# Clustered attention into a SiLU feed-forward: reciprocals moved from VectorE to GpSimd as a power, and the first round's steps and the tail put in another order

## The chip, the cores and the metric

The kernel runs on one core of a Trainium2 chip. A core has engines that run at the same time, each with its own queue in program order: TensorE (PE, matmuls; PEld are its weight loads), VectorE (DVE), ScalarE (ACT) and GpSimd (POOL), and SP, whose queue here only issues transfers. The transfers themselves run on 16 DMA engines. Results of PE land in PSUM, in a few numbered slots; everything else lives in SBUF. The metric is device microseconds of one execution, median of three runs.

## The reference

Four batches of eight heads, 768 positions, 64 dimensions. Each query and key is assigned to one of 16 clusters; a query attends to the keys of its own cluster. The result goes through a feed-forward layer with SiLU, weights 512 x 2048 and 2048 x 512.

```python
q_assign = np.argmax(np.einsum('bhsd,hcd->bhsc', q_n, c_n), axis=-1)
k_assign = np.argmax(np.einsum('bhsd,hcd->bhsc', k_n, c_n), axis=-1)
mask = q_assign[:, :, :, None] == k_assign[:, :, None, :]
scores = np.where(mask, scale * np.matmul(q, k.transpose(0, 1, 3, 2)), -1000000000.0)
attn = np.exp(scores - np.max(scores, axis=-1, keepdims=True))
attn = attn / (np.sum(attn, axis=-1, keepdims=True) + 1e-09)
x = np.matmul(attn, v)                # then (batch*seq, heads*dim)
h = x @ w_in
out = (h * (1.0 / (1.0 + np.exp(-h)))) @ w_out
```

## The kernel before, in words

**Preparation of queries and keys.** They come as `items`: items 0 to 7 hold one head's keys and the first half of its queries, items 8 and 9 the second halves of batch 0's queries, items 10 on one head each. An item is loaded by SP (`load_qk`, L104; four buffers), split into a high half-precision part on ACT (`hi`, L136) and a low rest on DVE (`lo`, L142), and turned so that the dimension lies on partitions: items 0 to 7 by matmuls with the identity on PE (`pe_tr`, L154) and two copies, ACT's and DVE's (`tr_out`, L164), later ones by a transposing DMA that SP issues (`xpose`, L147). `logits` (L173) are matmuls with the normalised centroids; DVE finds the maximum and makes it one-hot (`am_t`, `am_max`), turns it back (`am_back`) and writes it as extra rows beside the turned queries and keys (`codes`, L230). So the mask comes out of the same matmul as the score.

**Steps.** The work is a list of 192 steps, 6 to a pass and 32 passes. In batch 0 a pass takes two heads and half of the queries (three steps per head), later one head and all queries. In step T the host issues the score matmuls of step T + 1 (`qk_mm`, L252; slot `st` of PSUM, two of them), any preparation on PE, feed-forward units, P times V of an earlier pass (`pv_mm`, L290; one slot), the exponential of step T on ACT (`exp`, L272), the copy out of P times V on DVE (`evac`, L302), and then what else the table `steps` has for T. `at(T, f, ...)` puts it there; within a step the order is that of the calls to `at`. Each engine follows this order, so a waiting instruction holds up all that stand behind it in its queue.

**The row sums' chain.** V carries 64 columns of ones, so P times V gives the row sums too. `evac` has SP spread the sums over 128 partitions (`zt`, 3 KB); `recip` (L315) inverts them on DVE and has SP store them to DRAM (`rzd`); `bcast` (L322) has SP load them back, repeated on 64 partitions (`rzb`, 192 KB); `norm` (L328) multiplies on GpSimd and leaves `xt`, the input of the feed-forward layer. E is the step of a pass's last `evac`: `recip` stands at E + 5, `bcast` at E + 7 and `norm` at E + 9 in batch 0 and the last pass, and one step later in the others.

**Feed-forward.** `unit_a` (L345) is four matmuls into `ph` and, one step later, a tanh on ACT and a product on DVE that leaves `gt`; `unit_b` (L365) is eight matmuls, half of one output tile. They wait in `qa` and `qb` until a batch's `xt` are due (`ready`, L553 and L556) and are mixed into the steps by `pop_mlp` (L386), and what is left comes in a loop after the last step (L586). The weights come in 16 loads that GpSimd issues (`w_load`), each behind a small copy (`pace`) that waits for a given step's exponential. `fill` (L394) issues matmuls on zeros that only keep PE busy.

Of the kernel before, what the change touches and what calls it, by code (L numbers as in the profile page):

```python
# [9 lines left out]
f32 = mybir.dt.float32  # L10
f16 = mybir.dt.float16
AF = mybir.ActivationFunctionType
ALU = mybir.AluOpType
# [4 lines left out]
def kernel(  # L18
# [10 lines left out]
    nc = tc.nc  # L29
    B, H, S, D = q.shape  # L30
# [4 lines left out]
    NJ = S // 128  # L35
    NFB = DF // 128
    NR = DM // 128
    NBH = B * H
# [6 lines left out]
    NSPLIT = H // 2  # L45
# [4 lines left out]
    const = ctx.enter_context(tc.tile_pool(name="const", bufs=1))  # L50
# [9 lines left out]
    ckl = const.tile([128, H, 32], f16, name="ckl")  # L60
    ohp = [const.tile([128, 12, 32], f16, name=f"oh{n}") for n in range(3)]
    ohn = [const.tile([128, 9, 32], f16, name=f"ohn{n}") for n in range(2)]
    pace = const.tile([128, 1], f32, name="pace")
    zz = const.tile([128, 512], f16, name="zz")

# [75 lines left out]
    @per_item  # L141
    def lo(n):  # L142
        ho, lw, src = parts(n)
        nc.vector.scalar_tensor_tensor(out=lw, in0=src, scalar=QS, in1=ho, op0=ALU.mult, op1=ALU.subtract)  # L144
# [9 lines left out]
    def pe_tr(n):  # L154
        hl = hls[n]
        trs[n] = []
        for a, w in ((0, NJ), (NJ, NJ // 2)):
            tag, bufs = ("po", 1) if a == 0 else ("mm", 2)
            pT = ps.tile([128, w * 128], f16, name="pT", tag=tag, bufs=bufs)
            for t in range(w):  # L160
                nc.tensor.transpose(pT[:, 128 * t : 128 * t + 128], hl[:, a + t].rearrange("p c d -> p (c d)"), ident)
            trs[n].append(pT)
# [9 lines left out]
    @per_item  # L172
    def logits(n):  # L173
        ab = abs_[n]
        if n < H:

            psL = ps.tile([128, 9, HC], f32, name="psL9", tag="mm", bufs=2)
            for t in range(9):
                for w, st in ((stk, True), (ckl, False)):
                    nc.tensor.matmul(psL[:, t, :], ab[:, t, :], w[:, order[n], 0:HC], start=st, stop=not st)  # L180
            psLs[n] = psL
            return
        psL = ps.tile([128, HALF], f32, name="psL", tag="mm", bufs=2)
        for w, st in ((stk, True), (ckl, False)):
            for g, (hd, _, _) in enumerate(items[n]):
                nc.tensor.matmul(  # L186
                    psL[32 * g : 32 * g + 32, :], w[:, hd % H, :],
                    ab[:, 3 * g : 3 * g + 3, :].rearrange("p n c -> p (n c)"),
                    start=st, stop=not st,
                )  # L190
        psLs[n] = psL
# [30 lines left out]
    @per_item  # L222
    def am_back(n):
        w = 32 * (9 if n < H else 12)
        ohT = mp.tile([128, HALF], f16, name="ohT", bufs=2)
        nc.vector.transpose(ohT[:, 0:w], oh_of(n).rearrange("p n c -> p (n c)"))  # L226
        ohs[n] = ohT
# [23 lines left out]

    def qk_mm(T):  # L252
        if not 0 <= T < NS:
            return
        p, j = divmod(T, NJ)
        pS = ps.tile([128, 1024], f32, name="pS", tag="st", bufs=2)
        if p < H:
            hd, a = head_of(p, j // 3), 3 * (p // NSPLIT)
            if T < 40 and T % 3 != 2:
                nc.tensor.matmul(pS[:, 0:512], zz[:, 0:128], zz, start=True, stop=True)  # L260
            for t in range(2):
                nc.tensor.matmul(  # L262
                    pS[:, 512 * t : 512 * t + HALF], k_tile(hd, 2 * (j % 3) + t), q_tiles(hd, a, 3),
                    start=True, stop=True,
                )
        else:
            lhsT = k_tile(p, j)
            nc.tensor.matmul(pS[:, 0:512], lhsT, q_tiles(p, 0, 4), start=True, stop=True)  # L268
            nc.tensor.matmul(pS[:, 512:768], lhsT, q_tiles(p, 4, 2), start=True, stop=True)  # L269
        pst[T] = pS  # L270

    def exp(T):  # L272
        if not 0 <= T < NS:
            return
        P = mp.tile([128, S], f16, name="P", bufs=12)
        pS = pst.pop(T)
        if T < NJ * H:
            nc.scalar.activation(  # L278
                out=P.rearrange("p (c x) -> p c x", c=2), in_=pS.rearrange("p (c x) -> p c x", c=2)[:, :, 0:HALF],
                func=AF.Exp, bias=0.0, scale=ESC,  # L280
            )
        else:
            nc.scalar.activation(out=P, in_=pS[:, 0:S], func=AF.Exp, bias=0.0, scale=ESC)  # L283
        Ps[T] = P
# [29 lines left out]

    def recip(p):  # L315
        rz = mp.tile([128, NJ], f32, name="rz", bufs=3)
        nc.vector.reciprocal(rz, zts.pop(p))
        rzd = drpool.tile([S], f32, name="rzd", tag="rzd", bufs=4)
        nc.sync.dma_start(rzd.rearrange("(p c) -> p c", c=NJ), rz)
        rzds[p] = rzd  # L320

    def bcast(p):  # L322
# [13 lines left out]
        )  # L336

    gts = {}
    late = []

    def flush():
        while late:
# [40 lines left out]
    qa, qb = [], []  # L383
# [9 lines left out]

    def fill(n):  # L394
        if n:
            junk = ps.tile([128, 512], f32, name="junk", tag="mm", bufs=2)
            for _ in range(n):
                nc.tensor.matmul(junk, zz[:, 0:128], zz, start=True, stop=True)

# [23 lines left out]
    def at(T, f, *a):  # L423
        steps.setdefault(T, []).append((f, a))
# [57 lines left out]
    nc.vector.tensor_copy(stk[0:64, :, 0:HC], chv)  # L482
    nc.vector.tensor_copy(stk[64:128, :, 0:HC], chv)
    nc.vector.tensor_copy(ckl[0:64, :, 0:HC], pst1[64:128, :].rearrange("d (h c) -> d h c", c=HC))
    fill(3)


    def due(n):
# [6 lines left out]
    for n in range(NI):  # L495
        d = due(n)
        near = n < H + 2
        if n < H:
            first = n == 0
            at(3 * n - 2 - 3 * first, codes, n)  # L500
            at(3 * n - 3 - 3 * first, am_max, n)
            at(3 * n - 3 - 3 * first, am_back, n)
            at(3 * n - 5 - first, logits, n)
            if n > 0:
                at(3 * n - 7, pe_tr, n)
                at(3 * n - 7, tr_out, n)
                at(3 * n - 10, lo, n)
            if n > 1:
                at(3 * n - 12, hi, n)
        else:  # L510
            at(d - 5, am_back, n)
            at(d - 5, codes, n)
            at(d - 6, am_max, n)
            at(d - 7, am_t, n)
            at(d - 8, logits, n)
            x = d - (14 if near else 23)
            at(x, xpose, n)
            at(x - 2, lo, n)
            at(x - 4, hi, n)
        if n > 3:  # L520
            at(d - (24 if near else 40), load_qk, n)
# [4 lines left out]
            at(T - (12 if n < H else 15), load_v, hd)  # L526
        at(T - 6, cast_v, hd)
    for n in range(2 * NW):
        T = 14 * n // 5 - 3

        def gated(T=T, n=n):
            if T > 0:
                nc.gpsimd.tensor_copy(pace, Ps[T][:, 0:1])
            w_load(n)

        at(T, gated)
# [3 lines left out]
    for p in range(NBH):  # L540
        for c in range(2):
            T = pass_at(p, c)
            pv_at[T] = (p, c, range(0, 3))
            pv_at[T + 1] = (p, c, range(3, 6))
            evac_at[T + 2] = (p, c)
        E = T + 2
        near = p < H or p == NBH - 1
        at(E + (5 if near else 6), recip, p)
        at(E + (7 if near else 8), bcast, p)
        N = E + (9 if near else 10)  # L550
        for c in range(2):
            at(N, norm, p, c)
        if p in (NSPLIT - 1, H - 1):  # L553
            ready[N + 3] = [(0, p // NSPLIT)]
        elif p % H == H - 1 and p < NBH - 1:
            ready[N + 3] = [(p // H, 0), (p // H, 1)]  # L556

    for T in range(min(steps), max(steps) + 1):
        p, j = divmod(T, NJ)
        for r in ready.get(T, []):  # L560
            qa.extend((*r, fb) for fb in range(NFB))
        done, late[:] = late[:], []
        qk_mm(T + 1)
        for f, a in steps.get(T, []):
            if f in on_pe:
                f(*a)
        if T >= 0:
            pop_mlp(j, 0.67 if T >= 114 else 0.43 if qb else 0.9)
        if T in pv_at:
            pv_mm(*pv_at[T])  # L570
        exp(T)
        if T in evac_at:
            evac(*evac_at[T])
        for f in done:
            f()
        for f, a in steps.get(T, []):
            if f not in on_pe:
                f(*a)
# [2 lines left out]

    tags = ("mm", "st")
    n = m = 0
    qa.extend((B - 1, 0, fb) for fb in range(NFB))
    qa.extend((B - 1, 1, fb) for fb in range(NFB))
    while qa or qb or late:  # L586
        if qa:
            unit_a(*qa.pop(0), tags[n % 2])
        if qb and (n % 5 in (1, 3) or not qa):
            unit_b(*qb.pop(0), ("po", "pv")[m // 2 % 2])  # L590
            m += 1
        n += 1
        while len(late) > (2 if qa or qb else 0):
            late.pop(0)()
# [28 lines left out]
```

## Time and profile before

| what | value |
|---|---|
| median of three runs | 381.83 us (380.72 to 383.01) |
| profiled execution, its own time | 380.09 us |
| span of that execution | 378.2 us |
| DVE reciprocals L317 | 32, 182 ns each |
| POOL normalisations L334 | 64, 1023 ns each in the mean |
| rzd and rzb together, us to landing (min, median, max) | 1.4, 3.3, 6.9 |
| zt, us to landing (min, median, max) | 2.0, 2.1, 4.7 |
| granted clock, 10 to 20 us | 0.50 |
| granted clock, 70 to 80 us | 0.65 |

An engine's share of busy time is over the whole span; the stages differ. The first 80 us hold the preparation of batch 0 and no feed-forward work; from there to 309 us attention steps and feed-forward units are mixed; after that only feed-forward work is left. A row of the timeline gives start, length, engine, line and operation, and in brackets how long the engine stood idle before it and what ended that. "SPq" rows are transfers being issued; they land later.

### The profile page before, as it was taken

The numbers are of one execution on the slowest core, as the hardware profiler recorded it, in microseconds if no ns is written. First come the engines' busy times: TensorE is split into PE (matmuls) and PEld (weight loads), VectorE is DVE, ScalarE is ACT, GpSimd is POOL, SyncE is SP. The second block draws the span as 40 slices with busy tenths as digits, with TensorE's granted clock in tenths as the row PEclk, the third lists the DMA queues.
The fourth block names the chain that finished last, engine by engine and source line by source line (L and its number), as shares of the span: only waits on it lengthen the run. The fifth ranks groups of instructions, "written<-read, shape, count | busy, mean of one in ns | idle before, by whom it ended". The sixth has DMA issues, their size and how long they took to land.

```text
span 378.2 us, 6204 instructions
## 1 busy us (share of the span) xinstructions
PE 340.9 (90%) x2130; PEld 179.4 (47%) x2130; DVE 257.7 (68%) x579; ACT 234.1 (62%) x367; POOL 97.4 (26%) x144
## 2 busy tenths in 40 slices
PE   6778878559999999999698899999999998899995
PEld 2445434225445554454354555555555554455542
DVE  5777867228896788878798887787667445454531
ACT  6566858438976678767787867677557623343310
POOL 5122253332430222234223232223321222200000
PEclk9588989869999999999999999999999999999999
DMA  6698788989965675569967655443211012010102
GB/s 180 135 218 180 152 118 171 195 179 165 197 156 134 118 177 143 144 155 193 213 104 176 128 126 155 112 112 86 71 52 49 23 50 97 2 55 29 52 32 83
DMA packets 74479, 46.51 MB, mean 123 GB/s; under 512 B 52944, under 2 KB 68304, under 8 KB 74448
## 3 DMA queue, kind: packets, MB, share of 16 engines
q1 hardware_dynamic: 71120, 41.93, 45.9%
q0 software_dynamic: 3328, 4.20, 7.7%
q8 instruction: 16, 0.26, 0.3%
q14 instruction: 15, 0.12, 0.1%
HBM read 33.59 MB, written 6.39 MB: 106 GB/s over the span
## 4 chain that ended last, share of the span: by engine, by line
PE 63%; DVE 19%; DMA 9%; issue 3%; ACT 2%; SPq 2%; POOL 0%; DVEq 0%; ACTq 0%; POOLq 0%
PE po L371 21%; PE ph L352 16%; PE pO L300 12%; PE pS L268 5%; DVE gt L357 3%; DMA zt<-osb 3%; PE pS L269 3%; DMA qk<-in_q_dram 3%; DVE osb L306 2%; PE psL L186 2%; DMA rzb<-rzd 2%; DVE ab L248 2%; PE pS L262 2%; DVE ohT L226 2%; DVE ab L246 2%
## 5 line engine op out<-in xcount | busy, mean ns | idle before, releaser
L283 ACT ACTIVATE P<-pS 128x768 f16<-128x768 f32 x144 | 115.5, 812 | 52.8 <-PE pS L269 52.5
L334 POOL TENSOR_TENSOR xt<-osb,rzb 64x384 f16<-64x384 f32 x64 | 64.4, 1023 | 195.6 <-DMA rzb<-rzd 157.7
L352 PE MATMUL ph<-xt,win_s 128*128 128x384 f16 x512 | 101.9, 328 | 10.0 <-POOL xt L334 7.4
L300 PE MATMUL pO<-P,vt 128*128 128x384 f16 x384 | 85.8, 333 | 8.1 <-DVE osb L306 8.1
L356 ACT ACTIVATE tn<-ph 128x384 f32<-128x384 f32 x128 | 62.6, 489 | 47.5 <-PE ph L352 46.8
L357 DVE SCALAR_TENSOR_TENSOR gt<-tn,ph 128x384 f16<-128x384 f32 x128 | 69.6, 547 | 31.2 <-ACT tn L356 28.1
L371 PE MATMUL po<-wout_s,gt 128*128 128x512 f16 x384 | 89.7, 379 | 0.0
L352 PEld LDWEIGHTS <-win_s 128*128 128x128 f16 x512 | 49.9, 97 | 45.8 <-issue 11.1
L306 DVE COPY osb<-pO 128x384 f32<-128x384 f32 x64 | 35.3, 551 | 34.1 <-PE pO L300 30.9
L371 PEld LDWEIGHTS <-gt 128*128 128x128 f16 x384 | 37.5, 98 | 40.9
L300 PEld LDWEIGHTS <-vt 128*128 128x128 f16 x384 | 35.8, 99 | 41.7 <-issue 20.9
L268 PE MATMUL pS<-ab 80*128 80x512 f16 x144 | 54.8, 381 | 0.3
L278 ACT ACTIVATE P<-pS 128x768 f16<-128x768 f32 x48 | 37.1, 809 | 12.5 <-PE pS L262 11.7
L269 PE MATMUL pS<-ab 80*128 80x256 f16 x144 | 38.9, 270 | 0.0
L144 DVE SCALAR_TENSOR_TENSOR hl<-qk,hl 128x768 f16<-128x768 f32 (+1 forms) x34 | 30.6, 901 | 1.5 <-ACT hl L139 1.2
L378 DVE TENSOR_SCALAR ot<-po 128x512 f32<-128x512 f32 x24 | 16.5, 689 | 18.4 <-PE po L371 18.3
L139 ACT ACTIVATE hl<-qk 128x768 f16<-128x768 f32 (+1 forms) x34 | 27.2, 802 | 1.9 <-DMA qk<-in_q_dram 1.9
L197 DVE STREAM_TRANSPOSE LT<-psL 128x384 f32<-128x384 f32 x26 | 15.1, 579 | 11.1 <-PE psL L186 10.6
L127 POOL CAST vt<-vn 128x384 f16<-128x384 f32 x32 | 16.7, 523 | 17.9 <-DMA vn<-in_v_dram 17.2
L269 PEld LDWEIGHTS <-ab 80*128 80x128 f16 x144 | 14.2, 99 | 11.2 <-issue 0.8
L268 PEld LDWEIGHTS <-ab 80*128 80x128 f16 x144 | 14.0, 97 | 11.1 <-issue 0.3
L248 DVE TENSOR_SCALAR ab<-ohT 16x384 f16<-16x384 f16 x48 | 18.2, 379 | 1.1
(74 smaller groups left out, 226.3 us busy)
## 6 DMA issues: line engine op xcount, KB each, us to landing
qk<-in_k_dram SPq DMA_DIRECT2D x32, 192.0 KB, 3.3
vn<-in_v_dram SPq DMA_DIRECT2D x32, 192.0 KB, 3.4
rzb<-rzd SPq DMA_DIRECT2D x32, 192.0 KB, 3.5
out_dram<-ot SPq DMA_DIRECT2D x24, 256.0 KB, 2.1
qk<-in_q_dram SPq DMA_DIRECT2D x24, 192.0 KB, 3.1
win_s<-in_moe_w_in_dram POOLq DMA_DIRECT2D x8, 256.0 KB, 5.0
wout_s<-in_moe_w_out_dram POOLq DMA_DIRECT2D x8, 256.0 KB, 5.9
qk<-in_q_dram SPq DMA_DIRECT2D x16, 96.0 KB, 3.3
```

What stands on the lines that cost most here:

```text
L144: nc.vector.scalar_tensor_tensor(out=lw, in0=src, scalar=QS, in1=ho, op0=ALU.mult, op1=ALU.subtract)
L268: nc.tensor.matmul(pS[:, 0:512], lhsT, q_tiles(p, 0, 4), start=True, stop=True)
L269: nc.tensor.matmul(pS[:, 512:768], lhsT, q_tiles(p, 4, 2), start=True, stop=True)
L278: nc.scalar.activation(out=P.rearrange("p (c x) -> p c x", c=2), in_=pS.rearrange("p (c x) -> p c x", c=2)[:, :, 0:HALF], func=AF.Exp, bia ...
L283: nc.scalar.activation(out=P, in_=pS[:, 0:S], func=AF.Exp, bias=0.0, scale=ESC)
L300: nc.tensor.matmul(pOs[p, c], vts[hd % H][:, j, :], rhs, start=(j == 0), stop=(j == NJ - 1))
L306: nc.vector.tensor_copy(osb[:, c * HALF : c * HALF + HALF], pOs.pop((p, c)))
L334: nc.gpsimd.tensor_tensor(out=xts[b % 2][h // 2][o : o + 64, T0 : T0 + HALF], in0=osbs[p][o : o + 64, cs], in1=rzbs[p][o : o + 64, cs], op ...
L352: nc.tensor.matmul(ph, win_s[:, r, ts(fb, 128)], xts[b % 2][r][:, T0 : T0 + HALF], start=(r == 0), stop=(r == NR - 1))
L356: nc.scalar.activation(out=tn, in_=ph, func=AF.Tanh, bias=0.0, scale=0.5)
L357: nc.vector.scalar_tensor_tensor(out=gt[:, fb, :], in0=tn, scalar=1.0, in1=ph, op0=ALU.add, op1=ALU.mult)
L371: nc.tensor.matmul(po, gt[:, fc, ts(t, 128)], wout_s[:, fc, :], start=(fc == 0), stop=(fc == NFB - 1))
```

## The change

The reciprocal becomes a power of -1 on GpSimd, with a constant tile of -1, and its store to DRAM a step of its own (`rz_out`). The chain's steps are now E + 4, E + 5, E + 8 and E + 11 for all passes but the last, where all stand at E. The feed-forward units of a batch start two to four steps later than before. Head 0's logits, one-hot and codes are written out ahead of the step loop, with head 1's transposes in between; heads 1 to 7 get their maximum, codes, transposes and low parts in steps that differ from each other. The scores of steps 0 to 2 and their exponentials are issued two steps earlier. `fill` uses the scores' PSUM slots and is called once in each of the steps -6 to -1. The weight loads stand 5/2 steps apart rather than 14/5. After the last step, the units of the last batch are held until the older ones are used up.

```diff
+    neg = const.tile([128, NJ], f32, name="neg")
+    nc.gpsimd.memset(neg, -1.0)
...
     def recip(p):
         rz = mp.tile([128, NJ], f32, name="rz", bufs=3)
-        nc.vector.reciprocal(rz, zts.pop(p))
+        nc.gpsimd.tensor_tensor(out=rz, in0=zts.pop(p), in1=neg, op=ALU.pow)
+        rzs[p] = rz
+
+    def rz_out(p):
         rzd = drpool.tile([S], f32, name="rzd", tag="rzd", bufs=4)
-        nc.sync.dma_start(rzd.rearrange("(p c) -> p c", c=NJ), rz)
+        nc.sync.dma_start(rzd.rearrange("(p c) -> p c", c=NJ), rzs.pop(p))
         rzds[p] = rzd
...
     def fill(n):
         if n:
-            junk = ps.tile([128, 512], f32, name="junk", tag="mm", bufs=2)
+            junk = ps.tile([128, 1024], f32, name="junk", tag="st", bufs=2)[:, 0:512]
...
-    fill(3)
+    lo(1)
+    logits(0)
+    pe_tr(1)
+    am_max(0)
+    am_back(0)
+    codes(0)
+    tr_out(1)
...
         if n < H:
-            first = n == 0
-            at(3 * n - 2 - 3 * first, codes, n)
-            at(3 * n - 3 - 3 * first, am_max, n)
-            at(3 * n - 3 - 3 * first, am_back, n)
-            at(3 * n - 5 - first, logits, n)
             if n > 0:
-                at(3 * n - 7, pe_tr, n)
-                at(3 * n - 7, tr_out, n)
-                at(3 * n - 10, lo, n)
+                at(3 * n - 3, am_back, n)
+                at(3 * n - 3, codes, n)
+                at(3 * n - 4, am_max, n)
+                at(3 * n - 5, logits, n)
             if n > 1:
+                at(3 * n - 8, tr_out, n)
+                at(3 * n - 9, pe_tr, n)
+                at(3 * n - 11, lo, n)
                 at(3 * n - 12, hi, n)
...
-        T = 14 * n // 5 - 3
+        T = 5 * n // 2 - 4
...
-            if T > 0:
+            if T in Ps:
...
-        near = p < H or p == NBH - 1
-        at(E + (5 if near else 6), recip, p)
-        at(E + (7 if near else 8), bcast, p)
-        N = E + (9 if near else 10)
+        last = p == NBH - 1
+        at(E + (0 if last else 4), recip, p)
+        at(E + (0 if last else 5), rz_out, p)
+        at(E + (0 if last else 8), bcast, p)
+        N = E + (0 if last else 11)
         for c in range(2):
             at(N, norm, p, c)
         if p in (NSPLIT - 1, H - 1):
-            ready[N + 3] = [(0, p // NSPLIT)]
+            ready[N + 5] = [(0, p // NSPLIT)]
         elif p % H == H - 1 and p < NBH - 1:
-            ready[N + 3] = [(p // H, 0), (p // H, 1)]
+            ready[N + 4] = [(p // H, 0), (p // H, 1)]
...
-        qk_mm(T + 1)
+        if T >= 2 or T < 0:
+            qk_mm(T + 1 if T >= 2 else T + 3)
         for f, a in steps.get(T, []):
             if f in on_pe:
                 f(*a)
-        if T >= 0:
+        if T < 0:
+            fill(1 if T >= -6 else 0)
+        else:
             pop_mlp(j, 0.67 if T >= 114 else 0.43 if qb else 0.9)
...
-        exp(T)
+        if T >= 3 or T < 1:
+            exp(T if T >= 3 else T + 2)
...
-    qa.extend((B - 1, 0, fb) for fb in range(NFB))
-    qa.extend((B - 1, 1, fb) for fb in range(NFB))
-    while qa or qb or late:
+    last = [(B - 1, c, fb) for c in range(2) for fb in range(NFB)]
+    while qa or qb or late or last:
+        if not qa and not qb and len(late) < 2:
+            qa, last = last, []
         if qa:
             unit_a(*qa.pop(0), tags[n % 2])
```

More of the change, by code (lines that the diff above doesn't have):

```diff
@@ L338 @@
     gts = {}
-    late = []
+    late, rzs = [], {}
     def flush():
```

## The prediction

> **What bounds the kernel now.** I read the busy table and the forty slices first, then the same sums by stretch, then the waits, and then the timeline around each gap of TensorE (PE). The first fence is the page's parts 1 and 2 and the answer for three stretches (length, then busy time per engine and number of instructions, then the granted clock and the DMA share).
>
> ```profile
> PE 340.9 (90%) x2130; PEld 179.4 (47%) x2130; DVE 257.7 (68%) x579; ACT 234.1 (62%) x367; POOL 97.4 (26%) x144
> ...
> PE   6778878559999999999698899999999998899995
> ...
> PEclk9588989869999999999999999999999999999999
> DMA  6698788989965675569967655443211012010102
> ...
> 0.00:80.00 80.00, 58.91 (x444) 31.41 (x445) 49.38 (x137) 49.56 (x69) 28.34 (x60) 0.83 0.83 175
> 80.00:300.00 220.00, 210.10 (x1308) 111.11 (x1308) 172.83 (x378) 161.83 (x252) 62.65 (x78) 0.99 0.58 131
> 300.00:374.25 74.25, 71.85 (x380) 36.93 (x378) 34.78 (x64) 22.76 (x47) 6.40 (x7) 1.00 0.13 48
> ```
>
> After 80 us the kernel is bound by PE: 9.9 us idle in 220 us, 2.4 us in the next 74. Before 80 us PE idles 21.1 us and runs part of the time at half clock. All feed-forward work waits until attention has been normalised, so an idle microsecond of PE early in the run is not made up later. What the change can win is idle PE (37.3 us in all, 4.0 of them the output's drain after the last matmul) and slow clock. The next fence is the timeline at the gaps (start, length, engine, line; in brackets the idle time before, and what ended it).
>
> ```profile
> 15.46 0.81 ACT L278 ACTIVATE P<-pS 128x768 f16<-128x768 f32 x1
> ...
> 26.17 0.84 ACT L139 ACTIVATE hl<-qk 128x768 f16<-128x768 f32 x1 [0.66 <-DMA qk<-in_q_dram]
> ...
> 27.77 0.48 PE L262 MATMUL pS<-gt 96*128 96x384 f16 x2 [1.91 <-ACT P L278]
> ...
> 49.32 0.82 PE L262 MATMUL pS<-abk 96*128 96x384 f16 x2 [3.02 <-DVE abk L240]
> ...
> 72.55 0.19 DVE L317 RECIPROCAL rz<-zt 128x6 f32<-128x6 f32 x1 [6.83 <-DMA zt<-osb]
> ...
> 73.22 1.12 PE L300 MATMUL pO<-P,vt 128*128 128x384 f16 x3 [4.30 <-DVE osb L306]
> ...
> 79.09 0.48 PE L352 MATMUL ph<-xt,win_s 128*128 128x384 f16 x1 [3.47 <-POOL xt L334]
> ...
> 186.19 0.32 PE L352 MATMUL ph<-xt,win_s 128*128 128x384 f16 x1 [1.59 <-POOL xt L334]
> ...
> 318.87 1.95 PE L352 MATMUL ph<-xt,win_s 128*128 128x384 f16 x11 [0.52 <-DVE gt L357]
> ...
> 322.66 2.92 PE L352 MATMUL ph<-xt,win_s 128*128 128x384 f16 x17 [1.84 <-POOL xt L334]
> ```
>
> At 72.55 the reciprocal on VectorE (DVE) has stood 6.83 us waiting for the row sums, with the copy that frees pO queued behind it, so PE stood too. The three L352 rows are feed-forward units whose normalised input was late.
>
> **The change, part by part.**
>
> *Reciprocals on GpSimd.* 32 reciprocals of 182 ns (L317: 5.8 us) and 7.1 us of waiting leave DVE; 32 two-input instructions and one memset join POOL. No row shows a power. The lowest bound is the 128x1 cast L533, 0.19 us; the nearest two-input row, L334, takes 0.99 us for 64x384. I take 0.5 us and keep 0.19 to 0.99: 16 us more on an engine busy 97 of 378. What waits for zt now stands on POOL, and behind it there are the previous pass's two normalisations, the cast of V, and the paced weight loads. The copy that frees pO is no longer behind it. SP's store of rz waits for POOL instead of DVE, ahead of zt of the next pass, a V load and rzb; there is room, since the reciprocal that ended near 63.1 us was stored only at 67.21, SP being busy with a transpose (2.16 us) and two loads.
>
> But the stall does not vanish with it. The first unit needs four xt, and the last of them comes from a chain on SP that runs back to back from 50.8 us:
>
> ```profile
> 62.69 0.47 SPq L325 DMA_DIRECT2D rzb<-rzd  x1
> 63.68 2.16 SPq L150 DMA_TRANSPOSE ab<-hl  x1
> 65.89 0.58 SPq L114 DMA_DIRECT2D qk<-in_k_dram  x1
> 66.53 0.58 SPq L114 DMA_DIRECT2D qk<-in_q_dram  x1
> 67.21 0.52 SPq L319 DMA_DIRECT2D rzd<-rz  x1
> 67.83 1.50 SPq L310 DMA_DIRECT2D zt<-osb  x1
> 69.38 0.58 SPq L123 DMA_DIRECT2D vn<-in_v_dram  x1
> 72.32 0.48 SPq L325 DMA_DIRECT2D rzb<-rzd  x1
> ```
>
> One pass takes 72.32 - 62.69 = 9.6 us there, and SP's order is the same in the changed kernel up to pass 8. PE's stalls on this chain are 4.30 + 3.47 + 0.47 (a second wait at 80.05) = 8.24 us. Without the first, PE reaches the first unit sooner and waits there. The later start (step 42 for 38) gives it four steps to do meanwhile, and they come off the end. Bounds: nothing and 8.2 us; I take 1.0, because the chain's own end moves only with the round before it.
>
> *First round.* codes(0) ended at 12.22 on DVE, yet the first exponential began at 15.46, after logits(1) on PE and the copy L168 on ScalarE. Now scores(0) follow codes(0): a filler and two matmuls (13.23 for 0.85 us here) and exp(0) at about 13.6. That is 1.9 us, but group two waits for codes(1), which follow the same DVE work: bounds 0 and 1.9, taken 1.0. The early lo frees the qk buffers a step sooner, and one weight load goes out near 8 us, where the DMA share was 0.39 (8 to 12 us), not at 14.44; so the load that held hi at 26.17 should land earlier: bounds 0 and 1.91, taken 1.0. PE's waits on codes (L240) add up to 3.5 + 1.1 = 4.6 us; codes now stand two steps ahead of their scores, and those of head 7 go ahead of item 8's, which took 0.54 + 1.05 us of DVE just before: bounds 0 and 4.6, taken 3.0. Against this, the fillers: six in the loop for three dropped, three more of 0.43 us at half clock, or 1.3 us, and now in the scores' two PSUM slots, where one can wait for an exponential (0.81 us) with the transposes and logits queued behind it on PE. If the clock rises sooner (the granted clock was 0.5 in every stretch from 8 to 20 us, and PE works on this path), each 3.4 us sooner give half of that back: bounds -1.7 and +2.1, taken +0.6 us.
>
> *Weights.* 16 loads in steps -4 to 33, before -3 to 39. Behind POOL's first normalisation (49.6 us) there were eight; ten now stand ahead of it. Each costs about 29/16 = 1.8 us of all DMA engines (queue q0: 7.7% of 378 us). Between the first and fourth normalisation there are six both ways. Two loads more before 50 us, where the DMA share leaves about a fifth free; I cost them at nothing. If that cover is gone, it is 3.6 us on the chain above.
>
> *Later chains.* From pass 8, reciprocal and rz store come earlier by two and one steps, the broadcast stays, units start two steps later. That gap at 186.19 is 1.59 us, and two steps there took 1.6 us (ACT at 0.81 us each): taken 1.6, bounds 0 and 1.6. Steps without filler cost nothing: PE has 0.65 us of scores, 0.43 of P times V and 0.12 of logits in a step, more than ACT's 0.81 plus 0.14.
>
> *Tail.* The last pass's chain is issued at once, and batch 3's units wait until all older ones are used up. Before, PE lost 0.52 + 1.84 us. The chain from the last copy (309.2) is zt 2.1, power 0.5, rzd 1.9, rzb 3.5 and, since pass 30's rzb is now behind it on SP, four normalisations: about 12 us. Beside it stand 11 units (0.65) and 10 half products (1.73), 24 us. Bounds 0 and 2.4, taken 2.3. If that cover fails, the 2.4 come back.
>
> Sum: 1.0 + 1.0 + 1.0 + 3.0 + 1.6 + 2.3 - 0.6 = 9.3 us; less 0.5 for DVE work held by POOL's new instructions: 8.8. The profiled execution took 380.09 us (span 378.2, 1.9 around it): 371.3. The median of the runs is 1.7 above it: **373.0 us**.
>
> The 0.5 is from this pair of rows, 0.25 us at their median but far longer beside a normalisation:
>
> ```profile
> L248 DVE TENSOR_SCALAR ab<-ohT x48: 250/252/1053, 85.0 to 288.3; 16x384 f16<-16x384 f16 x48
> ```
>
> Beside that row stands the Trainium skill, SBUF — State Buffer, section Who interferes with whom: a DVE instruction in a two-port mode or with two SBUF inputs and a GpSimd one exclude each other for a whole instruction. It speaks against this change: were each power of 0.5 us to block DVE fully, that would be 16 us of DVE, and the sum would fall to nothing if all of it lay on the path. The trace agrees on the lock, but DVE is not the bound after 80 us. GPSIMD Engine Reference, section Engine selection, puts elementwise work on VectorE at half the time; by it the power would be an estimated 0.36 us and the sum the same.
>
> **Rivals.** *The first round gives nothing:* the DMA share is 0.83 up to 80 us, and if the transfers set the pace there, steps in better order wait just the same. For it: the 9.6 us period on SP. Against it: the waits on L240, which no transfer ended. Then the late terms stay, 1.6 + 2.3 = 3.9 us: 378. *The chain shortens too:* rz no longer waits for DVE (the reciprocal at 87.24 came late), two weight loads fewer are behind the fourth normalisation; six of the 8.2 us go as well: 367. *Slower, by transfers ahead of the first norms:* the 3.6 us of two weight loads and 0.5 us a head for seven heads (fillers waiting for score slots at half clock) are 7.1, less 3.9 of late gains: 385. It decides from 3.9 us. *Slower, by a long power:* POOL does 2.5 us per pass (two L334, one cast) in 8.7 us (144 steps of L283, first start 91.4, last 299.5, six to a pass); beyond 6.2 us a power makes POOL the bound. At 8 us: 31 x 1.8 = 56, less the gains, about 430. No row speaks for it; none excludes it. *The change does not do what it says* would be one where DVE still stands: its copy still waits for P times V only, so I give it nothing apart.
>
> **Numbers.** Forecast 0.50, first round nothing 0.19, chain too 0.13, slow transfers 0.12, slow power 0.06. About 0.5%, 1.9 us, is what a measurement here can tell. Faster: 0.50 + 0.13 + 0.14 of the 0.19 = 0.77; same: the other 0.05 and 0.01 of slow transfers = 0.06; slower 0.17. The range leaves out the slow power and little on each side: 364 to 387; the forecast's own is 369 to 377.
>
> **What would show it.** A power near 0.5 us; no DVE wait on zt; PE waiting once, near step 42, for xt; L240 waits under 2 us; exp(0) near 13.6; no PE gap at 186 or 320. I am wrong if PE idles over 21 us before its first unit, or if the power passes some 3 us, the room that SP left it.

## The result and the profile after

The changed kernel takes 367.39 us (median of four runs, 363.97 to 368.98); the kernel before, run beside it, 381.97 us (380.72 to 383.01). The ratio is 0.9608 with a 95% interval of 0.9524 to 0.9691, so it is faster. The profiled execution took 368.89 us, of which 367.1 are its span: 11.1 us less than the span before. TensorE gives 7.2 of them by idling less (30.1 for 37.3 us, span less busy time) and 3.9 by shorter busy time. First the page's parts 1 and 2 of the changed kernel, then its sums by stretch, in the same columns as the views of the kernel before.

```profile
PE 337.0 (92%) x2133; PEld 178.0 (48%) x2133; DVE 251.6 (69%) x547; ACT 235.5 (64%) x367; POOL 144.3 (39%) x177
...
PE   7979698369989999999989999999999999999995
...
PEclk9998999859999999999999999999999999999999
DMA  6799899988756666677657774433211102100102
```

```profile
0.00:80.00 80.00, 59.59 (x468) 32.12 (x469) 53.41 (x142) 53.44 (x75) 38.20 (x72) 0.92 0.92 182
80.00:300.00 220.00, 214.26 (x1335) 113.45 (x1334) 167.31 (x353) 161.42 (x251) 100.91 (x102) 1.00 0.54 130
300.00:363.00 63.00, 63.00 (x334) 32.41 (x331) 30.21 (x52) 20.62 (x42) 5.14 (x5) 1.00 0.13 49
```

By stretch, PE's idle time went from 21.1 to 20.4 us before 80 us, from 9.9 to 5.7 up to 300 us, and from 2.4 to nothing until its last matmul. The first 80 us hardly idle less, yet 24 more matmuls ran in them (three of them fillers), at a mean clock of 0.92 for 0.83. The timeline around the gaps shows what was won (one answer for each engine, put in order of time):

```profile
13.02 0.81 ACT L280 ACTIVATE P<-pS 128x768 f16<-128x768 f32 x1 [0.71 <-PE pS L264]
...
24.12 0.84 ACT L141 ACTIVATE hl<-qk 128x768 f16<-128x768 f32 x1 [2.56 <-DMA qk<-in_q_dram]
...
25.71 0.48 PE L264 MATMUL pS<-gt 96*128 96x384 f16 x2 [2.32 <-ACT P L280]
...
43.91 1.50 ACT L280 ACTIVATE P<-pS 128x768 f16<-128x768 f32 x2
...
59.78 1.35 POOL L319 TENSOR_TENSOR rz<-zt,neg 128x6 f32<-128x6 f32 x1 [0.85 <-DMA zt<-osb]
...
64.09 0.41 SPq L324 DMA_DIRECT2D rzd<-rz  x1
...
72.06 0.48 SPq L330 DMA_DIRECT2D rzb<-rzd  x1
...
72.34 1.34 POOL L319 TENSOR_TENSOR rz<-zt,neg 128x6 f32<-128x6 f32 x1 [3.98 <-DMA zt<-osb]
...
75.48 1.95 POOL L339 TENSOR_TENSOR xt<-osb,rzb 64x384 f16<-64x384 f32 x2 [1.80 <-DMA rzb<-rzd]
...
76.52 0.48 PE L357 MATMUL ph<-xt,win_s 128*128 128x384 f16 x1 [9.28 <-POOL xt L339]
...
77.47 0.48 PE L357 MATMUL ph<-xt,win_s 128*128 128x384 f16 x1 [0.47 <-POOL xt L339]
```

The first exponential starts at 13.02 us (15.46 before). The load for `hi` still comes last, but at 24.12 instead of 26.17, and the scores behind it start 2.06 us earlier. The 22nd exponential starts at 43.91; before, it came at 50.24, behind the 3.02 us wait on codes, which is gone. Then the three waits on late row sums have become one (9.28 us, and 0.47 right behind it): PE has nothing to do from 67.24 to 76.52, since the first unit's third and fourth `xt` hang on the fourth pass's chain. Its power runs at 59.78; the row at 72.34 is the power of the next pass, where the wait on zt now stands. SP, which has a transpose and two loads ahead of it, stores the fourth pass's rz at 64.09, and the view of the chain that ended last gives what follows as the landing of that store (start and length):

```profile
64.09 7.95 DMA rzd<-rz
```

Only then, at 72.06, can rzb be issued, and the two `norm` follow at 75.48. Before, the store went out 3.12 us later (67.21) and rzb 5.11 us behind it. PE resumes 2.57 us earlier than before (76.52 for 79.09), and by then the exponential of step 44 has run (at 67.0); before, that of step 41 was the last, at 75.1. The gaps at 186 and 320 us have no counterpart.

The power is dearer than thought. This is the answer for the tile `rz`:

```profile
L319 POOL TENSOR_TENSOR rz<-zt,neg x32: 1317/1333/1453, 33.7 to 299.9; 128x6 f32<-128x6 f32 x32
...
  DMA zt<-osb: 53.1, 18
who waited for it (us, times):
  DVE osb L308: 1.2, 1
```

1333 ns in the median, against 182 ns for the reciprocal on DVE, for six elements a partition. GpSimd stands 53.1 us waiting for zt (18 times) and is busy 144.3 us (97.4 before); by the profile DVE waited for it once, 1.2 us.

### The profile page after: what moved, and what is told of

It is laid out like the page before. It is cut to its first block, busy times and chain, and to the rows that moved or that the text cites. A ratio compares the mean times of both kernels' runs of the same rounds, so it can differ in the third digit from the quotient of the medians.

```text
span 367.1 us, 6191 instructions
## 1 busy us (share of the span) xinstructions
PE 337.0 (92%) x2133; PEld 178.0 (48%) x2133; DVE 251.6 (69%) x547; ACT 235.5 (64%) x367; POOL 144.3 (39%) x177
## 4 chain that ended last, share of the span: by engine, by line
PE 64%; DMA 13%; DVE 13%; SPq 4%; issue 2%; POOL 2%; ACT 2%; DVEq 0%; ACTq 0%; POOLq 0%
PE ph L357 21%; PE po L376 20%; PE pO L302 11%; DMA rzd<-rz 5%; PE pS L270 5%; DMA ab<-hl 3%; PE pS L271 3%; DVE gt L362 3%; PE psL L188 2%; DVE hl L146 2%; DMA qk<-in_q_dram 2%; SPq L152 2%; DMA rzb<-rzd 2%; DVE osb L308 2%; SPq L116 1%
## 5 line engine op out<-in xcount | busy, mean ns | idle before, releaser
L285 ACT ACTIVATE P<-pS 128x768 f16<-128x768 f32 x144 | 115.7, 812 | 48.5 <-PE pS L271 48.3
L357 PE MATMUL ph<-xt,win_s 128*128 128x384 f16 x512 | 100.3, 327 | 11.5 <-POOL xt L339 9.8
L339 POOL TENSOR_TENSOR xt<-osb,rzb 64x384 f16<-64x384 f32 x64 | 66.3, 1054 | 87.3 <-DMA rzb<-rzd 73.3
L362 DVE SCALAR_TENSOR_TENSOR gt<-tn,ph 128x384 f16<-128x384 f32 x128 | 70.4, 550 | 25.7 <-ACT tn L361 22.3
L302 PE MATMUL pO<-P,vt 128*128 128x384 f16 x384 | 84.2, 328 | 3.4 <-DVE osb L308 3.4
L319 POOL TENSOR_TENSOR rz<-zt,neg 128x6 f32<-128x6 f32 x32 | 43.4, 1358 | 53.5 <-DMA zt<-osb 53.1
L302 PEld LDWEIGHTS <-vt 128*128 128x128 f16 x384 | 35.0, 97 | 33.7 <-issue 13.2
L280 ACT ACTIVATE P<-pS 128x768 f16<-128x768 f32 x48 | 37.3, 809 | 8.3 <-PE pS L264 8.0
L146 DVE SCALAR_TENSOR_TENSOR hl<-qk,hl 128x768 f16<-128x768 f32 (+1 forms) x34 | 32.5, 959 | 2.1 <-ACT hl L141 1.8
L129 POOL CAST vt<-vn 128x384 f16<-128x384 f32 x32 | 18.4, 575 | 14.9 <-DMA vn<-in_v_dram 14.2
```

What stands on the lines that cost most here:

```text
L302: nc.tensor.matmul(pOs[p, c], vts[hd % H][:, j, :], rhs, start=(j == 0), stop=(j == NJ - 1))
L319: nc.gpsimd.tensor_tensor(out=rz, in0=zts.pop(p), in1=neg, op=ALU.pow)
L339: nc.gpsimd.tensor_tensor(out=xts[b % 2][h // 2][o : o + 64, T0 : T0 + HALF], in0=osbs[p][o : o + 64, cs], in1=rzbs[p][o : o + 64, cs], op ...
L357: nc.tensor.matmul(ph, win_s[:, r, ts(fb, 128)], xts[b % 2][r][:, T0 : T0 + HALF], start=(r == 0), stop=(r == NR - 1))
L362: nc.vector.scalar_tensor_tensor(out=gt[:, fb, :], in0=tn, scalar=1.0, in1=ph, op0=ALU.add, op1=ALU.mult)
```

## The experiments

Each kernel had three timed rounds beside the kernel before, on the same chip. Unless said otherwise, an edit is made to the changed kernel.

### The engine of the reciprocal

```diff
-        nc.gpsimd.tensor_tensor(out=rz, in0=zts.pop(p), in1=neg, op=ALU.pow)
+        nc.vector.reciprocal(rz, zts.pop(p))
```

> The changed kernel with the reciprocal back on VectorE at the changed kernel's steps (E + 4); all else as changed. Order theory (the record's: the round's order, the later chains and the tail give the gain, the engine of the reciprocal about 1 us): 367 to 371 us, VectorE waits on zt some 7 to 15 us in all, the wait before the first feed-forward unit shrinks by what VectorE now stands. Engine theory (the freed VectorE is the main gain): 375 or more.

365.01 us (362.81 to 365.95), ratio 0.9566 (0.9499 to 0.9632). So no gain shows that comes from GpSimd. If anything the power costs some 2 us, which the intervals don't separate. The timeline of PE with the reciprocal on DVE:

```profile
61.13 1.12 PE L302 MATMUL pO<-P,vt 128*128 128x384 f16 x3 [2.57 <-DVE osb L308]
...
69.15 0.65 PE L302 MATMUL pO<-P,vt 128*128 128x384 f16 x3 [1.23 <-DVE osb L308]
...
74.03 0.32 PE L357 MATMUL ph<-xt,win_s 128*128 128x384 f16 x1 [1.32 <-POOL xt L339]
...
75.00 0.32 PE L357 MATMUL ph<-xt,win_s 128*128 128x384 f16 x1 [0.65 <-POOL xt L339]
```

The stalls of DVE are back, but small: 2.57 + 1.23 and then 1.97 us on xt. In all PE waits 6.3 us for DVE's copies (osb) and 2.0 for xt, against 3.4 and 9.8 in the changed kernel. Both hang on the same transfers, but here the fourth pass's store of rzd landed 3.62 us after its issue, there 7.95; what decides that is not shown.

Then the other half alone, the power in the kernel before, with its old steps:

```diff
-        nc.vector.reciprocal(rz, zts.pop(p))
+        nc.gpsimd.tensor_tensor(out=rz, in0=zts.pop(p), in1=neg, op=ALU.pow)
```

> The kernel before with only the reciprocal moved to GpSimd, same steps. Order theory: 380 to 383 us; VectorE's 6.8 us wait on zt is gone, TensorE's 4.3 us gap near 69 us is gone, and the wait before the first feed-forward unit grows from 3.9 to about 8 us. Engine theory: 372 to 376.

438.61 us (437.11 to 439.4), ratio 1.15 (1.1428 to 1.1572): a plain miss, 57 us slower, with GpSimd busy a third of the time. Of this kernel, the page's part 1 and the timeline of POOL and SP over one pass (a transpose and two loads of SP are left out between 147 and 151.49):

```profile
PE 352.6 (81%) x2130; PEld 182.3 (42%) x2130; DVE 252.5 (58%) x547; ACT 235.5 (54%) x367; POOL 142.8 (33%) x177
```

```profile
143.57 2.06 POOL L336 TENSOR_TENSOR xt<-osb,rzb 64x384 f16<-64x384 f32 x2 [10.82 <-DVE mx L215]
...
145.60 1.38 POOL L319 TENSOR_TENSOR rz<-zt,neg 128x6 f32<-128x6 f32 x1
...
147.00 0.33 SPq L321 DMA_DIRECT2D rzd<-rz  x1
...
151.49 0.48 SPq L327 DMA_DIRECT2D rzb<-rzd  x1
...
155.17 1.97 POOL L336 TENSOR_TENSOR xt<-osb,rzb 64x384 f16<-64x384 f32 x2 [7.80 <-DMA rzb<-rzd]
...
157.21 1.32 POOL L319 TENSOR_TENSOR rz<-zt,neg 128x6 f32<-128x6 f32 x1
```

In the old steps `norm` of pass p (E + 9 in batch 0, E + 10 later) stands ahead of the reciprocal of pass p + 1 (E + 6 + 5, later E + 6 + 6). With both on GpSimd the queue closes a loop: norm(p) waits for rzb(p); only behind it comes power(p + 1), which rzd(p + 1), rzb(p + 1) and norm(p + 1) wait for. (The bracket of the first row names a reduction on DVE, which `norm` doesn't read; that of the second names rzb.) So this pass takes the whole round trip, 155.17 - 143.57 = 11.6 us, though GpSimd works 3.9 of them (2.06 + 1.38 + a cast of 0.49). In the changed kernel six steps take 8.95 us there (the exponentials of steps 71 and 95 start at 115.7 and 151.5). The thirteen passes from 143.57 to 288.37 take 11.1 us each, the ten after them 8.4 to 10.1, and the last exponential starts at 353.1 for 299.5 in the kernel before: 53.6 of the 57 us. In the new steps the power of pass p + 1 (E + 10) stands ahead of norm(p) (E + 11): one step apart.

To see that this order is what saves the changed kernel, `norm` is put two steps earlier, with the units left at their steps:

```diff
-        N = E + (0 if last else 11)
+        N = E + (0 if last else 9)
...
-            ready[N + 5] = [(0, p // NSPLIT)]
+            ready[N + 7] = [(0, p // NSPLIT)]
...
-            ready[N + 4] = [(p // H, 0), (p // H, 1)]
+            ready[N + 6] = [(p // H, 0), (p // H, 1)]
```

> The changed kernel with one thing moved: the normalisation of a pass at E + 9 instead of E + 11, so that on GpSimd it stands ahead of the next pass's power (E + 10), not behind it; the feed-forward units start at the same steps. Loop theory (power, store, broadcast and normalisation then form one closed chain from pass to pass, about 1.4 + 8 + 2 = 11.5 us a pass against 8.7): 420 to 440 us, with waits of TensorE for xt of over 5 us in batches 1 to 3. Rival (the loss of the power alone came from storing at the same step on SP's queue, not from GpSimd's order): 365 to 371 us.

427.66 us (423.5 to 429.51), ratio 1.1229 (1.1093 to 1.1365). Its `norm` start 11.6 us apart, as above, though the store of rz has its own step here, so the rival falls:

```profile
144.99 1.95 POOL L339 TENSOR_TENSOR xt<-osb,rzb 64x384 f16<-64x384 f32 x2 [7.32 <-DMA rzb<-rzd]
147.03 1.92 POOL L319 TENSOR_TENSOR rz<-zt,neg 128x6 f32<-128x6 f32 x1
...
156.59 2.06 POOL L339 TENSOR_TENSOR xt<-osb,rzb 64x384 f16<-64x384 f32 x2 [7.19 <-DVE osb L308]
```

The changed kernel itself, run again on that chip, took 366.55:

> The changed kernel once more, as the mark on this chip for the runs beside it. 364 to 369 us.

That one gave 365.01 to 368.07, ratio 0.9624 (0.9522 to 0.9726). And the same move of `norm` with the reciprocal on DVE:

> The same move of the normalisation to E + 9, but with the reciprocal on VectorE. Loop theory: no closed chain on one queue, so within 1% of the changed kernel, 362 to 368 us. Rival (an early normalisation is bad by itself): 380 or more.

365.28 us (362.89 to 367.69), ratio 0.9625 (0.9517 to 0.9734). Neither the move alone nor the power in the new place costs anything that the intervals show, and together they cost 61 us. The loop is shown.

### The first round

The old first round in the changed kernel (head 0's steps back in the loop, the old steps of heads 1 to 7, scores and exponentials not ahead, three fillers):

```diff
-    lo(1)
-    logits(0)
...
-    tr_out(1)
+    fill(3)
...
-        if T >= 2 or T < 0:
-            qk_mm(T + 1 if T >= 2 else T + 3)
+        qk_mm(T + 1)
```

> The changed kernel with batch 0's preparation, the first scores and the fillers as before; the power, the later chains, the weights and the tail stay changed. Order theory: 4 to 7 us slower than the changed kernel, 371 to 375, with half clock on TensorE again between 8 and 22 us and more waits on codes. Engine theory: within 1.5 us of the changed kernel.

373.84 us (373.28 to 375.41), ratio 0.9812 (0.9749 to 0.9875): the round is worth about 0.02 of the time here (0.9812 less 0.9608 or 0.9624), 7 to 8 us, give or take some 4 (half widths added in squares). In PE's timeline the wait on codes is back; those on `hi`'s load and on the fourth pass's xt are there as in the changed kernel (2.32 and 9.28 us):

```profile
28.81 0.48 PE L264 MATMUL pS<-gt 96*128 96x384 f16 x2 [3.06 <-ACT P L280]
...
52.61 0.82 PE L264 MATMUL pS<-abk 96*128 96x384 f16 x2 [5.26 <-DVE abk L242]
...
81.44 0.48 PE L357 MATMUL ph<-xt,win_s 128*128 128x384 f16 x1 [5.43 <-POOL xt L339]
```

The reverse, the new round alone in the kernel before (the reciprocal on DVE; chain, weight loads and tail old):

```diff
+    lo(1)
+    logits(0)
...
+    tr_out(1)
...
+        if T >= 2 or T < 0:
+            qk_mm(T + 1 if T >= 2 else T + 3)
```

> The kernel before with only the first round changed (head 0 written out, heads 1 to 7 in steps of their own, first scores early, fillers); reciprocal on VectorE, chain steps, weights and tail as before. Order theory: most of the gain, 370 to 374 us, with the tail's gap of 2.4 us and the 1.6 us gap at batch 1 still there. Rival (the round needs the later chain steps, since VectorE's wait on zt eats what it won): 376 to 380.

377.26 us (374.89 to 381.08), ratio 0.9865 (0.9793 to 0.9937): about 5 us (2.7 either way), less than the theory's and in the rival's band. PE's timeline shows what the round alone leaves in place (line numbers of the old chain):

```profile
70.80 1.12 PE L300 MATMUL pO<-P,vt 128*128 128x384 f16 x3 [3.14 <-DVE osb L306]
...
76.45 0.48 PE L352 MATMUL ph<-xt,win_s 128*128 128x384 f16 x1 [3.26 <-POOL xt L334]
...
315.75 1.95 PE L352 MATMUL ph<-xt,win_s 128*128 128x384 f16 x11 [0.52 <-DVE gt L357]
...
319.57 2.92 PE L352 MATMUL ph<-xt,win_s 128*128 128x384 f16 x17 [1.88 <-POOL xt L334]
```

Then without the six fillers in the loop:

```diff
-            fill(1 if T >= -6 else 0)
+            pass
```

> The changed kernel without the six filling matmuls in steps -6 to -1. If they keep TensorE's clock up: half clock again for some 3 to 13 us before 25 us, exp(3) later than 18.1 by 1 to 3 us, 369 to 372 us. If the early clock is full for another reason: 365 to 368 us.

366.88 us (365.16 to 367.31), ratio 0.9638 (0.9558 to 0.9718): the fillers are worth nothing that can be measured, neither as a cost nor for the clock.

Last, the wait on `hi`'s load at 25.71 us: with the reciprocal on DVE, `hi` and `lo` of items 8 and 9 later, so that ScalarE doesn't stand before the load:

```diff
-            at(x - 2, lo, n)
-            at(x - 4, hi, n)
+            at(x - (1 if near else 2), lo, n)
+            at(x - (2 if near else 4), hi, n)
```

> The changed kernel with the reciprocal on VectorE and, for items 8 and 9, the high part two steps later and the low part one step later (just ahead of their transposing transfer). The gap of 2.1 to 3.4 us near 23 us, where ScalarE stands before the exponential of step 6 for item 8's load, should go: 361 to 364 us. If another wait takes its place: as e1, 365.

366.57 us (363.49 to 369.74), ratio 0.9578 (0.949 to 0.9667), against 0.9566 without the edit: nothing. In its profile (of the longest of its runs, so its times are not compared) the gap near 23 us is gone, and PE waits 5.45 us at 34.8 us for the transposed item instead: the wait seems to have moved from the reader of the load to what comes of it.

### The chain's steps, the later start and the tail

The chain's old places and the old start of the units, with round, weight loads and tail new, and the reciprocal on DVE:

```diff
-        at(E + (0 if last else 4), recip, p)
-        at(E + (0 if last else 5), rz_out, p)
-        at(E + (0 if last else 8), bcast, p)
-        N = E + (0 if last else 11)
+        near = p < H
+        at(E + (0 if last else 5 if near else 6), recip, p)
+        at(E + (0 if last else 5 if near else 6), rz_out, p)
+        at(E + (0 if last else 7 if near else 8), bcast, p)
+        N = E + (0 if last else 9 if near else 10)
...
-            ready[N + 5] = [(0, p // NSPLIT)]
+            ready[N + 3] = [(0, p // NSPLIT)]
...
-            ready[N + 4] = [(p // H, 0), (p // H, 1)]
+            ready[N + 3] = [(p // H, 0), (p // H, 1)]
```

> The changed kernel with the reciprocal on VectorE and the old places of the row sums' chain (E + 5 and E + 7 and E + 9 in batch 0, one later in the others) and the old, earlier start of the feed-forward units (three steps behind the normalisation); first round, weight loads and tail stay new. Theory (the new places and the later start give what the first round alone did not, 377.3 against 365.0 us): 371 to 374, with PE waiting on xt L339 again for over 1.5 us near 186 us or behind a VectorE wait on zt over 4 us near 70 us. Rival (the earlier weight loads and the rest give it): 364 to 367. Together they would be between, 368 to 370.

375.15 us (374.04 to 379.26), ratio 0.9871 (0.9749 to 0.9992), against 0.9566 with the new places: 0.0305, or 11.7 us of 382, give or take 5.3 (the half widths 0.0122 and 0.0067, added in squares). Its PE timeline, and the sums of 60 to 80 us of this kernel and then of the first experiment's, which has the new places:

```profile
61.50 1.12 PE L302 MATMUL pO<-P,vt 128*128 128x384 f16 x3 [5.66 <-DVE osb L308]
...
74.76 0.48 PE L357 MATMUL ph<-xt,win_s 128*128 128x384 f16 x1 [4.78 <-POOL xt L339]
...
183.09 0.32 PE L357 MATMUL ph<-xt,win_s 128*128 128x384 f16 x1 [1.41 <-POOL xt L339]
```

```profile
60.00:80.00 20.00, 13.19 (x60) 6.21 (x60) 6.10 (x13) 8.19 (x12) 6.19 (x9) 0.70 0.99 200
```

```profile
60.00:80.00 20.00, 15.53 (x91) 7.82 (x91) 11.58 (x23) 12.47 (x19) 6.18 (x8) 0.91 1.01 201
```

The transfers go at the same pace in both: DMA share 0.99 and 1.01, and the reciprocals that wait for zt start at 60.82 and 68.00 here, at 60.45 and 68.47 there. The first unit's third xt is there at 74.76 and at 74.03. What differs is how much PE has ahead of each wait: 91 matmuls run in these 20 us instead of 60, at a mean clock of 0.91 for 0.70. PE idles 22.0 us here and 15.3 there before 80 us, and 11.9 and 6.1 from 80 to 300 us. Whether the places or the later start give more was not told apart.

The tail's edits undone (last chain at E + 5, 5, 7 and 9, and the old loop after the last step):

```diff
-    last = [(B - 1, c, fb) for c in range(2) for fb in range(NFB)]
-    while qa or qb or late or last:
-        if not qa and not qb and len(late) < 2:
-            qa, last = last, []
+    qa.extend((B - 1, 0, fb) for fb in range(NFB))
+    qa.extend((B - 1, 1, fb) for fb in range(NFB))
+    while qa or qb or late:
```

> The changed kernel with the last pass's chain at E + 5, 5, 7, 9 and the closing loop as before. Order theory: the gap of TensorE near the tail comes back, 2.4 us: 369 to 371. Rival (the tail's gap would have been hidden anyhow by the later leftovers): 367 to 368.

364.41 us (363.95 to 368.16), ratio 0.9551 (0.9483 to 0.962), and no gap of PE after 300 us: the edit is worth nothing that shows here. By the order of issue the later start leaves more older units over, and they would cover the last chain in the old order too; the start was not tried alone. The kernel with the old chain, the old start and the new tail has no gap of 1.8 us there either, so either side is enough.

### A later start of the first units

The one wait of 9.28 us has the transfers behind it, so PE needs more work ahead of it: the first units start at step 50, not 42.

```diff
-            ready[N + 5] = [(0, p // NSPLIT)]
+            ready[N + (13 if p < H - 1 else 5)] = [(0, p // NSPLIT)]
```

> The changed kernel (power on GpSimd) with the first feed-forward units at step 50 rather than 42. If TensorE's wait of 6.7 to 9.3 us for xt near 67 us is a matter of position, the scores of steps 45 to 49 fill it and full clock is kept: 360 to 364 us. If the transfers of the chain also hold up queries, keys and V, the wait moves to another instruction and the time stays at 365 to 369.

362.15 us (361.62 to 363.96), ratio 0.9485 (0.9422 to 0.9548); its slowest run lies just below the fastest of the changed kernel's eight (363.97). Against the changed kernel's 0.9608 that is 0.0123 less, give or take 0.0105; from the kernel with the reciprocal on DVE (0.9566) it is not told apart. Its sum for the first 80 us:

```profile
0.00:80.00 80.00, 64.88 (x504) 34.70 (x505) 58.80 (x154) 59.24 (x82) 39.00 (x72) 0.95 0.90 184
```

36 matmuls more than in the changed kernel, PE busy 5.3 us longer, at a clock of 0.95 for 0.92. PE's largest wait in its whole span is 3.0 us, on the exponential behind `hi`'s load.

## Why the prediction was right, and where not

The forecast was 373.0 us; the time is inside its range, but 5.6 us below the point and outside the forecast's own 369 to 377. The direction and most places were right, the sizes were not, and the share of GpSimd was misjudged.

- *First round, 1.0 + 1.0 + 3.0 - 0.6 = 4.4 us.* Right, somewhat small. The scores behind `hi` start 2.06 us earlier, just what exp(0) and the load were to give; the 22nd exponential starts 6.3 us earlier. The runs give 5 us for the round alone and 7 to 8 when it is taken back, with some 3 to 4 us either way. Only the waits on codes were undervalued: PE's waits on L242 are 0.4 us (4.6 before). The idle wait on `hi` did not shrink (2.32 us for 1.91): the load lands earlier, and so does ScalarE's turn.
- *Merged stall, 1.0 us.* Here a step failed: "I take 1.0, because the chain's own end moves only with the round before it". The waits did merge, 9.28 + 0.47 us for 8.24, and the chain ended only 2.57 us earlier: rz was stored 3.12 us earlier, but rzb went out 7.97 us behind that store, for 5.11 before. The gain lies in the later start, whose four steps the prediction itself says "come off the end": three more are done by then, and at its 1.2 us of PE a step (0.65 + 0.43 + 0.12) that is an estimated 3.6 us. Between the old places and start and the new ones, both with the reciprocal on DVE, PE's idle time before 80 us fell by 6.7, so the upper bound, 8.2, was the nearer one.
- *Later chains, 1.6 us.* Mis-sized in the same way. The gap at 186 went as said, but PE's idle time from 80 to 300 us fell by 4.2, and by 5.8 between those two kernels. Both terms, 2.6 us together, were 11.7 (5.3 either way) in the runs. The rival "the chain shortens too" named the right time, 367, for another reason: PE's waits on the chain didn't shrink, so that agreement is luck.
- *Tail, 2.3 us.* The gap went, but with the tail's edits undone it is gone too, so the term can't be put down to them.
- *Weights, nothing.* Not tried alone. Round, new tail and weight loads together (0.9871) are no faster than the round alone (0.9865), so no gain of theirs shows.
- *DVE held by GpSimd, -0.5 us.* Neither shown nor refuted: the kernel with the reciprocal on DVE is 1.5 to 2.4 us faster in the medians, within the intervals, and its fourth pass's chain ends earlier as well. But the power's price was 1.33 us, outside the bounds of 0.19 to 0.99. It cost little, with GpSimd busy 39% of the span. Beside it stood the Trainium skill, GPSIMD Engine Reference, section Engine selection, which puts elementwise additions, products and maxima on VectorE, as GpSimd takes about twice as long; the prediction's estimate of 0.36 us from it is a quarter of the 1333 ns measured (7 times the reciprocal's 182), so the rule does not reach a power, and the measurement decides.
- *What the prediction did not see:* it moved the waits on zt to POOL, with "the previous pass's two normalisations" behind them, and asked whether POOL would be too busy (6.2 us a power). In the old steps those normalisations stand ahead, and the power there closes the loop and costs 57 us. The prediction's rival by a long power asked for the wrong quantity: not GpSimd's work in a pass, but the round trip through its queue.

Of the signs it named, exp(0) near 13.6 (13.02), no DVE wait on zt, one wait near step 42 (at step 44), L240 under 2 us and no gap at 186 or 320 held; the price of the power did not. The two signs of being wrong stayed away, the first of them narrowly: PE idles 19.9 us before the first unit gets its third xt, and the sign was 21.

## What to carry to other kernels

When an instruction moves to another engine's queue, write down the order there over two rounds: if it comes behind something that waits for the round trip which the previous round's own copy of it starts, each round takes the whole trip if that is longer than the round, however idle the engine is. Where a stage is paced by transfers, a reordering need not take its wait away; count how much independent work stands ahead of the wait. A gap that two edits close should be credited to neither until each has been taken back alone.

## What the hardware showed that was not expected

A power of six elements a partition takes 1.33 us on GpSimd, longer than the mean 1.05 us of a product with 384 elements a partition (L339): the size alone doesn't decide.

A store of 3 KB can set the pace. That of rzd takes 2.8 us to land in the median of the changed kernel, but 7.95 us at the place that PE waits for, 7.7 in the same kernel run again, and 3.62 with the reciprocal on DVE. The DMA share from 60 to 80 us was 1.02 in the changed kernel and 1.01 with the reciprocal on DVE, so it doesn't tell them apart. The cause stays open.

The clock's drop after a wait is a second price of it. These are the sums of 72 to 80 us, of the changed kernel and then of the one with the reciprocal on DVE (the granted clock is the last number but two):

```profile
72.00:80.00 8.00, 3.00 (x10) 1.25 (x10) 1.02 (x2) 1.57 (x3) 4.81 (x5) 0.50 0.78 155
```

```profile
72.00:80.00 8.00, 6.03 (x42) 3.10 (x40) 6.37 (x12) 5.50 (x10) 3.39 (x4) 1.00 0.97 204
```

Behind the long wait PE runs at half clock, and without it at full clock. The Trainium skill, TensorE: Matmul & The Clock Gate, Part 1, has the clock halve after some 3.4 us without work. The 9.28 us wait agrees: PE's last matmul before it ends at 67.24, and the granted clock is 1.00 from 70 to 71 us, 0.56 from 71 to 72 and 0.50 from 72 on. At the start it was less regular: from 8 to 20 us the granted clock was 0.50 in the kernel before, 1.00 in the changed kernel, 0.86 in the same kernel run again, and 1.00 without the loop's fillers. So the loop's fillers alone don't decide it, and what does was not settled.
